# Sliding-window attention with a gated mix: maxima and output blocks stored in one transfer each, attention features ordered by row number and then head, reciprocals as one repeated block

## The chip, the cores and the metric

The kernel runs on one core of one Trainium2 chip. The metric is the time of one execution on the device in microseconds (us); the smaller the better. A core has a matrix engine (PE, whose weight loads are shown apart as PEld), a vector engine (DVE), a scalar engine (ACT), a general engine (POOL) and a sequencer that here issues every transfer between the chip's memory (DRAM) and the core's memory (SP).

## The reference

`x` has 2048 rows (tokens) of 512 features. One branch is attention with 32 heads of 16 features, in which a token sees itself and the 255 tokens before it; the other is a gated feed-forward block with 1376 inner features. A gate of one number per token mixes the two.

```python
qkv = (x @ wqkv).reshape(B, S, 3, H, Dh)           # H = 32, Dh = 16
scores = jnp.einsum("bhqd,bhkd->bhqk", q, k) * (Dh ** -0.5)
mask = (idx[:, None] - idx[None, :] >= 0) & (idx[:, None] - idx[None, :] < 256)
p = softmax(where(mask, scores, -1e9)); o = einsum("bhqk,bhkd->bhqd", p, v)
a = o.reshape(B, S, D) @ wo
b = (sigmoid(x @ w_gate) * (x @ w_up)) @ w_down
out = g * a + (1 - g) * b                          # g = sigmoid((x * gate_w).sum(-1))
```

## The kernel before

All matrix products are made in float32 by splitting each operand into a high and a low part and adding three products (`mm3`, lines 88 to 91). The program has two long stages, which follow one another on PE.

**Attention (about 40 to 553 us).** The 32 heads form 8 groups of four, and each group has 16 blocks of 128 tokens, so that there are 128 units. The loop `for u in range(N)` (line 763) takes one unit per turn. In turn `u` the scores of unit `u` are computed once to find each query's maximum (`s_part`, line 331: PE at L340, DVE's maximum at L346). The scores of unit `u - 9` are computed a second time, transposed and with the maximum already subtracted (`st_part`, line 380: PE at L390, then ACT's exponential at L395). Between these, PE fills up with pieces of the projections and of the feed-forward block's first products (L273). Every fourth turn a burst of products with the values is done (`pv_burst`, L454).

The maximum travels from the first computation to the second through DRAM, once for four blocks, which gives 32 rounds. A round goes like this:

1. DVE splits the negated maxima into a high and a low part and transposes them in 32 x 32 squares into a tile `nt` of 128 x 32 (`max_split`, L358 to L362).
2. SP stores `nt` to `max_scratch` (`max_store`, L369): four transfers, one for each square of 32 partitions.
3. SP waits until these have landed and loads them back as rows of the operand tiles `ring` (`max_load`, L374). For round `s` this stands in turn 4s + 5.
4. `st_part` reads them, for the first time in turn 4s + 7 (in turn 4s + 9 where a group begins).

SP works through one list in order. What is issued in a turn is written in the loop: the load of maxima, then what the turn before has put into `later` (stores of computed tiles, L315), then up to three of the copies that build the next operand tile (`ring<-sh`, `ring<-sl`, also L315, `SD = 3`), then other loads; the store of maxima comes in the middle of the turn (L833). A transfer that has to wait holds up all those behind it.

**An output block.** After the last burst of a chunk of 512 tokens, `o_take` (line 462) holds four heads in a tile `ob` of 128 x 512: head `hh` has rows 32 hh to 32 hh + 31, of which the first 16 are the head's features and row 16 is the sum of the softmax (a column of ones stands beside the values). The rest is not used. Four transfers store the features to `oT_scratch` and a fifth stores the four rows of sums to `sum_scratch`.

**Down projection (about 553 us to the end).** For each chunk of 512 tokens (`c`) there are 11 steps (`f`), numbered `n` through all chunks, each of 12 matrix products `pd`; then 48 products `pa` with `wo` for the attention. A step reads a tile `hb`, which is made two to three steps ahead from two loads of `gu_scratch` (`h_load`, L686), a sigmoid (ACT, L703), a product (DVE, L704) and a split (`h_skew`; ACT at L85, DVE at L86). At the end of the attention loop `sums_load` (L713) reads the sums of a chunk, `sums_invert` takes the reciprocals (L717), and they are stored to `rec_scratch`. For each block of 128 tokens `o_load` (line 887) reads the features of all heads and their reciprocals. `o_scale` (line 895) spreads each head's reciprocal over the partitions of its 16 features with a shuffle (L897) and multiplies (L898).

Of the kernel before, what the change touches and what calls it, by code (L numbers as in the profile page):

```python
# [7 lines left out]
F32 = mybir.dt.float32  # L8
# [3 lines left out]
ALU = mybir.AluOpType  # L12
PSUM = bass.MemoryType.PSUM

P = 128
T = 2048
D = 512
ND = D // P
H = 32
DH = 16  # L20
HG = 4
NG = H // HG
CH = 512
NC = T // CH
# [26 lines left out]
QB = 32  # L51
# [12 lines left out]
def gated_mix_kernel(  # L64
# [14 lines left out]
    nc = tc.nc  # L79
# [10 lines left out]
        mm(ps, lh, rl, start=False, stop=False)  # L90
        mm(ps, ll, rh, start=False, stop=last)  # L91

    oT_d = nc.dram_tensor("oT_scratch", (D, T), F32, kind="Internal").ap()
    sum_d = nc.dram_tensor("sum_scratch", (NC, H, CH), F32, kind="Internal").ap()
    rec_d = nc.dram_tensor("rec_scratch", (NC, H, CH), F32, kind="Internal").ap()
    gu_d = nc.dram_tensor("gu_scratch", (2, NF, P, T), F32, kind="Internal").ap()
    v_d = nc.dram_tensor("v_scratch", (NB, P, VROW), F32, kind="Internal").ap()
# [39 lines left out]
    with ExitStack() as actx:  # L137
# [8 lines left out]
        later = []  # L146
# [218 lines left out]
        def max_store(s):  # L365
            nt = nms.pop(s)
            dst = max_d[s].rearrange("h l b (a t) -> a (h l b) t", t=QB)
            for a in range(P // QB):
                nc.sync.dma_start(dst[a], nt[a * QB:(a + 1) * QB])  # L369

        def max_load(s):
            st = ring[s // 2 % RING].bitcast(F32).rearrange("(a r) j f -> r a j f", r=QB)
# [89 lines left out]
        def o_take(g, i, n, acc):  # L462
            s = g * NC + i // 4
            if i % 4 == 0:
                obs[s] = cpool.tile([P, CH], F32, tag="ob", name=f"ob{s}", bufs=2)
            part = obs[s][:, i % 4 * P:(i % 4 + n) * P]
            lo = 64 if i == 0 else 0
            nc.scalar.copy(part, acc[0][:, 0:n * P])

            def rest():  # L470
                nc.vector.tensor_tensor(part[:, lo:], acc[1][:, lo:n * P], part[:, lo:], op=ALU.add)
                if (i + n) % 4:
                    return
                ob, c = obs.pop(s), i // 4
                for hh in range(HG):
                    h = g * HG + hh
                    later.append((oT_d[h * DH:(h + 1) * DH, c * CH:(c + 1) * CH], ob[32 * hh:32 * hh + DH]))
                later.append((sum_d[c, g * HG:(g + 1) * HG], ob.rearrange("(h r) f -> r h f", r=32)[DH]))

            behind.insert(0, rest)  # L480

# [78 lines left out]
        def gu_mm(f, c, w, k, half=None):  # L560
            fw = width(f, w)
            if (f, c, w) not in gp:
                gp[f, c, w] = ps.tile([P, CH], F32, tag="misc", name=f"gu{f}_{c}_{w}", bufs=3)
            wh, wl = (gv[:, 0, w], gv[:, 1, w]) if f < NF - 1 else wq[NG]
            group_mm(gp[f, c, w], fw, wh, wl, c, k, half)
# [17 lines left out]
        def proj_out(s):  # L583
# [5 lines left out]
                lambda k, h=None, a=(f, c, w): gu_mm(*a, k, h),  # L589
# [116 lines left out]
        sm = {}  # L706

        def flat(v, c):
            return v[c].rearrange("h (q t) -> (h q) t", t=P)

        def sums_load(c):
            sm[c] = cpool.tile([P, P], F32, tag="sm", name=f"sm{c}", bufs=2)
            nc.sync.dma_start(sm[c], flat(sum_d, c))  # L713

        def sums_invert(c):
            t = sm.pop(c)
# [39 lines left out]
        w = 0  # L756
# [6 lines left out]
        for u in range(N):  # L763
# [49 lines left out]
            for hh in range(HG):  # L813
                if hh == 0 and u % 2 == 0:
                    if u in bursts:
                        pv_burst(*bursts[u])
                if hh == 0:
                    head = min(2, bursts.get(u, (0, 0))[1] // 2)
                    run_slots(head)
                if u < NU:  # L820
                    s_part(u, hh)
                if 0 <= u - LAG < NU:
                    st_part(u - LAG, hh ^ 1 if u < NU else hh)
                if u < LAG:
                    flush(behind)
                    run_slots(GAP)
                    flush(acts)
                else:
                    if behind:
                        behind.pop(0)()  # L830
                    if acts:
                        acts.pop(0)()
                if hh == 2 and u % 4 == 0 and 0 < u <= NU:  # L833
                    max_store(u // 4 - 1)
                if u >= LAG:
                    run_slots((LAST[hh] if u >= NU else GAPS[u % 4][hh] if u > LAG + 2 else GAP * (u % 2 == 0 or hh < HG - 1)) - (hh < head))
# [10 lines left out]
            if SUMS <= u and (u - SUMS) % 4 == 0:  # L847
                sums_load((u - SUMS) // 4)
# [13 lines left out]
        def slot(h, d, c):  # L862
            return (xh, xl)[h][:, d, c * CH:(c + 1) * CH]

        def blocks(v):
            return v.rearrange("p (d t) -> p d t", d=ND)

        def free_slot(h, d, c):
            return slot(h, d, c).bitcast(F32)

        spread = [w - w % DH for w in range(QB)]
        oh = [blocks(slot(0, t, 1)) for t in range(4)]
        ol = [blocks(slot(1, t, 1)) for t in range(4)]
        o_raw = [blocks(free_slot(1, k, 2)) for k in range(2)]
# [1 line left out]
            region[:, SPARE + 3 * CH * k:SPARE + 3 * CH * (k + 1)].rearrange("p (n t) -> p n t", t=CH) for k in range(2)  # L876
        ]
        wide = [blocks(spare[k][:, 2]) for k in range(2)]
        rows = [blocks(free_slot(0, k, 3)) for k in range(2)]
        accs = [spare[k % 2][:, k // 2] for k in range(4)]  # L880

        def gate(c):
# [3 lines left out]

        def o_load(b):
            c, t = divmod(b, 4)
            nc.sync.dma_start(o_raw[b % 2], oT_d[:, b * P:(b + 1) * P].rearrange("(d p) t -> p d t", p=P))
            nc.sync.dma_start(  # L890
                rows[b % 2].rearrange("(h w) d t -> w h d t", w=DH)[0],
                rec_d[c, :, t * P:(t + 1) * P].rearrange("(d h) t -> h d t", d=ND),
            )

        def o_scale(b):
            o, w = o_raw[b % 2], wide[b % 2]
            nc.vector.stream_shuffle(w, rows[b % 2], spread)  # L897
            nc.vector.tensor_tensor(w, o, w, op=ALU.mult)  # L898

        def o_split(b):  # L900
            split(oh[b % 4], ol[b % 4], wide[b % 2])
# [1 line left out]
        for n, (c, f) in enumerate(steps):  # L903
# [22 lines left out]
            if 1 <= f < 9 and f % 2 == 1:  # L926
                o_load(4 * c + f // 2)
            if 3 <= f and f % 2 == 1:
                o_scale(4 * c + f // 2 - 1)
# [9 lines left out]
            for t in range(4):  # L939
                b = 4 * c + t  # L940
# [17 lines left out]
def _layout(inputs):  # L958
    import numpy as np

    x = np.asarray(inputs["A_x"]).reshape(T, D)
    wqkv = np.asarray(inputs["A_wqkv"])
    wqk = wqkv[:, :2 * D].reshape(ND, P, 2, NG, HG * DH).transpose(3, 1, 0, 2, 4).reshape(NG, P, ND, P)
    wg = np.asarray(inputs["B_w_gate"])
    wu = np.asarray(inputs["B_w_up"])
    nf = F // P
    gu = np.stack([wg, wu]).reshape(2, ND, P, F)
    main = gu[..., :nf * P].reshape(2, ND, P, nf, P).transpose(3, 0, 2, 1, 4)
    tail = gu[..., nf * P:].transpose(0, 2, 1, 3)
    last = np.concatenate([tail[1], tail[0, ..., :GL]], axis=2)  # L970
    return {
        "xT": x.T.reshape(ND, P, NC, CH).transpose(2, 0, 1, 3),
        "wqk": wqk,
        "wv": wqkv[:, 2 * D:],
        "wo": np.asarray(inputs["A_wo"]),
        "wgu": main,
        "wgu_last": last,
        "wg_last": tail[0, ..., GL:],
        "wd": np.asarray(inputs["B_w_down"]),
        "gw": np.asarray(inputs["gate_w"]).reshape(1, D),  # L980
        "x": x,
    }
# [23 lines left out]
```

## Time and profile before

| | |
|---|---|
| time, median of 3 runs | 721.82 us (721.75 to 722.55) |
| the profiled execution: its time / its span | 724.11 us / 722.4 us |
| PE busy | 715.6 us, 99% of the span |
| DVE / ACT / POOL busy | 66% / 60% / 24% |
| granted clock of PE | 1.0 of full speed in all slices |
| DMA engines, mean busy share | 54.5% of 16 engines' span by the SP queue's packets |

The span goes from the first to the last instruction of the profiled execution. An engine is busy while one of its instructions runs; the ends of matrix products are modelled, so that a busy PE may still hide short stalls.

### The profile page before, as it was taken

Reading aid. Unit: us, or ns where it says so; the run is one execution under the profiler, and the core shown is the slowest. Engines: PE = TensorE matmul, PEld = TensorE weight load, DVE = VectorE, ACT = ScalarE, POOL = GpSimd, SP = SyncE. Lnnn points to the kernel's source line nnn. Section 1 sums busy time; section 2 is a strip of 40 time slices with the busy share of each in tenths; the row PEclk is TensorE's granted clock in tenths of the full one; section 3 lists DMA queues with packets and bytes.
Section 4 is the critical chain, followed back from the end, with each engine's and each line's share of the span. In section 5 each row is a group of like instructions: output and inputs, shape, how many; then the busy total and the mean of one; then the engine's idle time right before and its main releaser. Section 6 shows DMA issues by size and latency. Waiting matters only on the chain.

```text
span 722.4 us, 20457 instructions
## 1 busy us (share of the span) xinstructions
PE 715.6 (99%) x7759; PEld 588.6 (81%) x7759; DVE 478.7 (66%) x1473; ACT 432.9 (60%) x889; POOL 169.9 (24%) x257
## 2 busy tenths in 40 slices
PE   9999999999999999999999999999999999999997
PEld 7689788888878888888788888888887888888886
DVE  5458777657766676766677667676566868576571
ACT  6413776667667677666667767767675635435241
POOL 7000333332233223333223323332331000000000
PEclk9999999999999999999999999999999999999999
DMA  9456554645355455443555525556475959377541
GB/s 325 106 155 196 162 131 125 164 134 153 97 137 150 124 145 146 136 133 98 140 162 138 139 88 161 162 152 201 161 238 183 311 185 317 147 242 234 174 115 59
DMA packets 89322, 117.93 MB, mean 163 GB/s; under 512 B 33870, under 2 KB 43726, under 8 KB 89224
## 3 DMA queue, kind: packets, MB, share of 16 engines
q1 hardware_dynamic: 89224, 116.62, 54.5%
q8 instruction: 61, 1.00, 0.6%
q14 instruction: 37, 0.30, 0.1%
HBM read 54.70 MB, written 36.71 MB: 127 GB/s over the span
## 4 chain that ended last, share of the span: by engine, by line
PE 99%; DMA 0%; issue 0%; DVE 0%; ACT 0%; DVEq 0%
PE gu L273 35%; PE pj L273 10%; PE pvs L454 8%; PE s L340 6%; PE st L390 6%; PE pd L89 6%; PE pd L91 6%; PE pd L90 6%; PE vps L254 4%; PE pa L89 2%; PE pa L91 2%; PE pa L90 2%; PE pvst L454 2%; PE gl L498 1%; PE vps L89 1%; PE vps L90 1%
## 5 line engine op out<-in xcount | busy, mean ns | idle before, releaser
L346 DVE CUSTOM_DVE_ANT_0 junk<-s,mask 128x384 f32<-128x384 f32 (+2 forms) x512 | 267.5, 531 | 142.8 <-PE st L390 92.1
L273 PE MATMUL gu<-xh,w 64*128 64x512 f32 x1264 | 330.9, 395 | 0.0
L395 ACT ACTIVATE region<-st 128x384 f32<-128x384 f32 (+2 forms) x512 | 242.6, 476 | 93.2 <-PE st L390 47.2
L273 PE MATMUL gu<-xl,w 64*128 64x512 f32 x632 | 225.7, 393 | 0.0
L273 PEld LDWEIGHTS gu<-xh,w 64*128 64x128 f32 x1264 | 188.0, 185 | 19.1 <-issue 6.1
L390 PE MATMUL st<-ring 64*128 64x384 f32 (+2 forms) x536 | 167.6, 320 | 1.2 <-DMA ring<-max_scratch 1.1
L340 PE MATMUL s<-ring 64*128 64x384 f32 (+2 forms) x536 | 167.8, 321 | 0.0
L400 POOL TENSOR_SCALAR_AFFINE_SELECT region<-region 128x512 f32<-128x512 f32 x128 | 86.8, 678 | 332.9 <-ACT region L395 293.8
L273 PEld LDWEIGHTS gu<-xl,w 64*128 64x128 f32 x632 | 113.8, 185 | 4.1
L340 PEld LDWEIGHTS s<-ring 64*128 64x128 f32 x536 | 98.6, 184 | 21.5 <-DVE mx L346 12.1
L390 PEld LDWEIGHTS st<-ring 64*128 64x128 f32 x536 | 98.3, 184 | 8.6 <-DMA ring<-max_scratch 1.4
L273 PE MATMUL pj<-xl,wqh 64*128 64x512 f32 (+1 forms) x240 | 95.5, 402 | 0.0
L273 PE MATMUL pj<-xh,wqh 64*128 64x512 f32 (+1 forms) x240 | 93.6, 395 | 0.0
L273 PE MATMUL pj<-xh,wql 64*128 64x512 f32 (+1 forms) x240 | 75.2, 392 | 0.0
L405 POOL TENSOR_SCALAR_AFFINE_SELECT region<-region 128x512 f32<-128x512 f32 x112 | 73.9, 660 | 0.0
L454 PE MATMUL pvs<-region,vg 64*32 64x320 f32 (+4 forms) x1408 | 71.5, 344 | 0.1
L454 PE MATMUL pvst<-region,vg 64*32 64x320 f32 (+4 forms) x1408 | 70.0, 340 | 0.0
L89 PE MATMUL pd<-ring,hb 128*128 128x512 f32 (+1 forms) x176 | 69.4, 395 | 0.0
L91 PE MATMUL pd<-ring,hb 128*128 128x512 f32 (+1 forms) x176 | 68.9, 392 | 0.0
L90 PE MATMUL pd<-ring,hb 128*128 128x512 f32 (+1 forms) x176 | 68.4, 389 | 0.0
L454 PEld LDWEIGHTS pvs<-region,vg 64*32 64x32 f32 x1408 | 44.4, 106 | 25.4 <-issue 4.2
L85 ACT CAST hb<-region 128x512 fp32r<-128x512 f32 (+1 forms) x36 | 22.4, 622 | 53.7 <-DVE region L704 41.4
(117 smaller groups left out, 1136.5 us busy)
## 6 DMA issues: line engine op xcount, KB each, us to landing
gu_scratch<-sp SPq DMA_DIRECT2D x79, 256.0 KB
region<-gu_scratch SPq DMA_DIRECT2D x68, 256.0 KB
ring<-sh SPq DMA_DIRECT2D x128, 128.0 KB
ring<-sl SPq DMA_DIRECT2D x64, 128.0 KB
guraw<-in_wgu_dram SPq DMA_DIRECT2D x20, 256.0 KB
v_scratch<-region SPq DMA_DIRECT2D x16, 272.0 KB
vg<-v_scratch SPq DMA_DIRECT2D x8, 544.0 KB
region<-in_xT_dram SPq DMA_DIRECT2D x16, 256.0 KB
```

What stands on the lines that cost most here:

```text
L89: mm(ps, lh, rh, start=first, stop=False)
L90: mm(ps, lh, rl, start=False, stop=False)
L91: mm(ps, ll, rh, start=False, stop=last)
L254: mm(vp[b], (xl if w == 1 else xh)[r, d, b * P:(b + 1) * P], (wvl if w == 2 else wvh)[r, d], start=k == 0 and half == 0, stop=k == 3 * ND ...
L273: mm(pt[0:fw], (wl if w == 2 else wh)[r, d], (xl if w == 1 else xh)[r, d, c * CH:(c + 1) * CH], start=k == 0 and half != 1, stop=k == 3 * ...
L340: mm(pt[:, (k - k0) * P:(e - k0) * P], lhsT, blk(g, k, hh, 1, e - k), start=k == k0, stop=e == i + 1, skip_group_check=True,)
L346: nc.vector.tensor_tensor_reduce(junk[:, 0:n], pt[:, 0:n], mask[:, 3 * P - n:], scale=1.0, scalar=NEG, op0=ALU.add, op1=ALU.max, accum_out ...
L390: mm(pt[:, (q - j) * P:(e - j) * P], lhsT, blk(g, q, hh, 0, e - q), start=q == j, stop=e == last, skip_group_check=True,)
L395: nc.scalar.activation(pts[u][:, hh, 0:n], pt[:, 0:n], AF.Exp, scale=SCALE)
L400: nc.gpsimd.affine_select(p[:, :, 0:P], p[:, :, 0:P], pattern=[[0, HG], [1, P]], compare_op=ALU.is_ge, fill=0.0, base=0, channel_multiplie ...
L405: nc.gpsimd.affine_select(p[:, :, 2 * P:], p[:, :, 2 * P:], pattern=[[0, HG], [-1, P]], compare_op=ALU.is_gt, fill=0.0, base=0, channel_mu ...
L454: mm(acc[half][32 * hh:32 * hh + 32, q0:q1], vr[r, c:c + 32], pts[g * NB + j][r, hh, q0 + o:q1 + o], start=m == 0, stop=m == len(order[0]) ...
```

## The change

The store of maxima is one transfer of all 128 partitions. An output block is stored in one transfer too: all 128 rows of `ob`, with the sums and the 15 unused rows of each head, into an `oT_scratch` that is now ordered by row number (0 to 31), then head, then token. The sums are row 16 of it, and `sums_load` reads them from there. In `o_load` a partition now holds one row number and one head (head = partition modulo 32), so that the reciprocals of a block of 128 tokens are the same 32 rows, repeated four times down the partitions and the same for all four tiles of features. They are loaded so, and the multiplication reads them with a repeated index; the shuffle goes. The rows of `wo` are put in the same order on the host.

```diff
-    oT_d = nc.dram_tensor("oT_scratch", (D, T), F32, kind="Internal").ap()
-    sum_d = nc.dram_tensor("sum_scratch", (NC, H, CH), F32, kind="Internal").ap()
+    oT_d = nc.dram_tensor("oT_scratch", (QB, H, T), F32, kind="Internal").ap()
...
             dst = max_d[s].rearrange("h l b (a t) -> a (h l b) t", t=QB)
-            for a in range(P // QB):
-                nc.sync.dma_start(dst[a], nt[a * QB:(a + 1) * QB])
+            nc.sync.dma_start(dst, nt)
...
                 ob, c = obs.pop(s), i // 4
-                for hh in range(HG):
-                    h = g * HG + hh
-                    later.append((oT_d[h * DH:(h + 1) * DH, c * CH:(c + 1) * CH], ob[32 * hh:32 * hh + DH]))
-                later.append((sum_d[c, g * HG:(g + 1) * HG], ob.rearrange("(h r) f -> r h f", r=32)[DH]))
+                dst = oT_d[:, g * HG:(g + 1) * HG, c * CH:(c + 1) * CH]
+                later.append((dst.rearrange("r h t -> h r t"), ob))
...
-            nc.sync.dma_start(sm[c], flat(sum_d, c))
+            nc.sync.dma_start(sm[c], oT_d[DH, :, c * CH:(c + 1) * CH].rearrange("h (q t) -> h q t", t=P))
...
-        rows = [blocks(free_slot(0, k, 3)) for k in range(2)]
+        rows = [free_slot(0, k, 3)[:, 0:P] for k in range(2)]
...
-            nc.sync.dma_start(o_raw[b % 2], oT_d[:, b * P:(b + 1) * P].rearrange("(d p) t -> p d t", p=P))
-            nc.sync.dma_start(
-                rows[b % 2].rearrange("(h w) d t -> w h d t", w=DH)[0],
-                rec_d[c, :, t * P:(t + 1) * P].rearrange("(d h) t -> h d t", d=ND),
-            )
+            heads = oT_d[0:DH].rearrange("r h t -> (r h) t")[:, b * P:(b + 1) * P]
+            nc.sync.dma_start(o_raw[b % 2], heads.rearrange("(d p) t -> p d t", p=P))
+            nc.sync.dma_start(rows[b % 2], rec_d[c, :, t * P:(t + 1) * P].partition_broadcast(P // H))
...
             o, w = o_raw[b % 2], wide[b % 2]
-            nc.vector.stream_shuffle(w, rows[b % 2], spread)
-            nc.vector.tensor_tensor(w, o, w, op=ALU.mult)
+            r, _ = bass.broadcast_tensor_aps(rows[b % 2].rearrange("p (o t) -> p o t", o=1), o)
+            nc.vector.tensor_tensor(w, o, r, op=ALU.mult)
...
-        "wo": np.asarray(inputs["A_wo"]),
+        "wo": np.asarray(inputs["A_wo"]).reshape(H, DH, D).transpose(1, 0, 2).reshape(D, D),
```

The order of the instructions on PE, ACT and POOL is the same as before. On SP the transfers keep their order and 224 of them go. These are SP's transfers before the change from the load of maxima of round 9 to that of round 10 (a row gives line, destination, source and shape, and how many in a row):

```order
L374 DMA ring<-max_scratch 4x2x512
L315 DMA gu_scratch<-sp_2_1_3131 128x512
L315 DMA ring<-fill_scratch 4x2x1024
L315 DMA ring<-sh_2739 32x1024 x2
L315 DMA gu_scratch<-sp_3_1_3192 128x512
L315 DMA ring<-sh_2739 32x1024 x3
L315 DMA oT_scratch<-ob_3260 16x512 x4
L315 DMA sum_scratch<-ob_3260 4x512
L315 DMA ring<-sh_2739 32x1024 x3
L315 DMA ring<-sl_2740 32x1024 x3
L538 DMA guraw_0_3402<-in_wgu_dram 128x512
L369 DMA max_scratch<-nt_3383 32x32 x4
```

The same place after the change:

```order
L372 DMA ring<-max_scratch 4x2x512
L314 DMA gu_scratch<-sp_2_1_3073 128x512
L314 DMA ring<-fill_scratch 4x2x1024
L314 DMA ring<-sh_2691 32x1024 x2
L314 DMA gu_scratch<-sp_3_1_3134 128x512
L314 DMA ring<-sh_2691 32x1024 x3
L314 DMA oT_scratch<-ob_3202 4x32x512
L314 DMA ring<-sh_2691 32x1024 x3
L314 DMA ring<-sl_2692 32x1024 x3
L534 DMA guraw_0_3340<-in_wgu_dram 128x512
L367 DMA max_scratch<-nt_3321 4x32x32
```

Five transfers of the block ahead of the store of maxima have become one, and so have the four of the store itself.

At the end of the attention loop, SP before the change issues the last output block, the last chunk's sums and the loads for step 5 and later ones:

```order
L315 DMA oT_scratch<-ob_10155 16x512 x4
L315 DMA sum_scratch<-ob_10155 4x512
L713 DMA sm_10281<-sum_scratch 128x128
L686 DMA region<-gu_scratch 128x512 x2
L123 DMA wdraw_10290<-in_wd_dram 128x512
```

After the change the load of sums reads what the one transfer has written, and so waits for all of it:

```order
L314 DMA oT_scratch<-ob_9935 4x32x512
L709 DMA sm_10057<-oT_scratch 128x1x128
L682 DMA region<-gu_scratch 128x512 x2
L122 DMA wdraw_10066<-in_wd_dram 128x512
L682 DMA region<-gu_scratch 128x512 x2
```

The loads of steps 5 and 6 stand behind it as before.

## Rows read from the trace of the kernel before

**Rows 1.** The page, span and part 1: busy time of each engine.

```profile
span 722.4 us, 20457 instructions
...
PE 715.6 (99%) x7759; PEld 588.6 (81%) x7759; DVE 478.7 (66%) x1473; ACT 432.9 (60%) x889; POOL 169.9 (24%) x257
```

**Rows 2.** Busy time by stretch: stretch, its length, PE, PEld, DVE, ACT, POOL, clock.

```profile
0.00:20.00 20.00, 18.75 (x80) 15.97 (x81) 9.27 (x15) 11.82 (x19) 13.77 (x13) 1.00 0.83 295
...
210.00:270.00 60.00, 58.87 (x810) 48.65 (x808) 40.64 (x150) 40.50 (x89) 19.46 (x30) 1.00 0.51 140
...
680.00:722.40 42.40, 38.11 (x167) 30.99 (x165) 20.68 (x36) 13.79 (x24) 0.00 (x0) 1.00 0.38 119
```

**Rows 3.** Chain that ended last, 200 to 216 us: start, us, what.

```profile
209.47 2.42 DMA ring<-max_scratch
```

**Rows 4.** Waits: engine, line, releaser; us in total, times, longest.

```profile
PEld st L390 <- DMA ring<-max_scratch: 1.4, 1, 1.4
```

**Rows 5.** Timeline of SP, rounds 9 to 10: start, us of issue, transfers.

```profile
198.00 1.91 SPq L315 DMA_DIRECT2D oT_scratch<-ob  x4
199.96 0.56 SPq L315 DMA_DIRECT2D sum_scratch<-ob  x1
...
204.62 0.34 SPq L538 DMA_DIRECT2D guraw<-in_wgu_dram  x1
205.08 1.78 SPq L369 DMA_DIRECT2D max_scratch<-nt  x4
209.47 0.59 SPq L374 DMA_DIRECT2D ring<-max_scratch  x1
```

**Rows 6.** Timeline of DVE: the transpose of round 10.

```profile
201.31 0.21 DVE L362 STREAM_TRANSPOSE nt<-nm 128x32 f32<-128x32 f32 x1
```

**Rows 7.** SP's issues by tensor: ns of one (least/median/most), first and last start.

```profile
L369 SPq DMA_DIRECT2D max_scratch<-nt x128: 302/419/2049, 59.3 to 518.3; - x128
L374 SPq DMA_DIRECT2D ring<-max_scratch x32: 552/582/596, 64.1 to 520.5; - x32
L315 SPq DMA_DIRECT2D oT_scratch<-ob x128: 302/420/1289, 89.5 to 555.5; - x128
L315 SPq DMA_DIRECT2D sum_scratch<-ob x32: 509/561/734, 91.2 to 556.0; - x32
```

**Rows 8.** Timeline of SP, round 17.

```profile
307.37 1.71 SPq L369 DMA_DIRECT2D max_scratch<-nt  x4
310.24 0.58 SPq L374 DMA_DIRECT2D ring<-max_scratch  x1
```

**Rows 9.** The page, part 3: packets, MB, share of 16 engines' span.

```profile
q1 hardware_dynamic: 89224, 116.62, 54.5%
```

**Rows 10.** Timeline of SP, round 3, and of PEld two turns later.

```profile
89.48 1.71 SPq L315 DMA_DIRECT2D oT_scratch<-ob  x4
...
94.06 1.73 SPq L424 DMA_DIRECT2D vg<-v_scratch  x2
...
103.04 0.58 SPq L374 DMA_DIRECT2D ring<-max_scratch  x1
...
105.31 0.18 PEld L390 LDWEIGHTS st<-ring 64*128 64x128 f32 x1
```

**Rows 11.** Timelines of SP, PE, ACT and DVE around the first steps.

```profile
553.16 0.50 PE L89 MATMUL pd<-ring,hb 128*128 128x512 f32 x1
554.23 1.69 SPq L315 DMA_DIRECT2D oT_scratch<-ob  x4
557.66 0.34 SPq L713 DMA_DIRECT2D sm<-sum_scratch  x1
561.68 0.63 ACT L703 ACTIVATE region<-region 128x512 f32<-128x512 f32 x1 [1.14 <-DMA region<-gu_scratch]
567.58 0.68 DVE L86 TENSOR_TENSOR hb<-region,hb 128x512 fp32r<-128x512 f32 x1
```

**Rows 12.** Groups by line on DVE: the shuffle of `o_scale`.

```profile
L897 DVE STREAM_SHUFFLE region<-xh 128x512 f32<-128x512 f32 x16 | 11.8, 739 | 0.0
```

More of the change, by code (lines that the diff above doesn't have):

```diff
@@ L869, in free_slot @@
             return slot(h, d, c).bitcast(F32)
-        spread = [w - w % DH for w in range(QB)]
         oh = [blocks(slot(0, t, 1)) for t in range(4)]
```

## Prediction

> **What bounds the kernel now.** I read the busy times first. PE is busy for 715.6 of 722.4 us, and no other engine comes near it [rows 1]. So only what PE waits for can shorten this kernel, and all of its idle time together is 6.8 us. The busy times by stretch say where these 6.8 us lie [rows 2]: 1.25 us before PE starts (20.00 - 18.75), 1.13 us between 210 and 270 us (60.00 - 58.87) and 4.29 us at the end (42.40 - 38.11), when PE has finished and the last rows are added and stored. That makes 6.67, and the rest, some 0.1 us, is spread thinly. The first and the last piece hold none of the changed lines. What can be won by taking waits from PE is therefore little more than the 1.13 us in the middle.
>
> The chain of work shows what this piece is: at 209.47 us it passes from PE to the load of maxima of round 10, which takes 2.42 us to land [rows 3]. The list of waits has the same event once: PE's weight load for the second scores waited 1.4 us for a load of maxima, and this is the only such wait [rows 4]. So 31 of the 32 rounds of maxima are in time and one is late.
>
> Why that one is late is told by SP. The transposed maxima of round 10 were ready at 201.31 + 0.21 = 201.52 us [rows 6], but their store was issued at 205.08, 3.56 us later, and the load at 209.47 [rows 5]. SP was behind: it came to the store only after an output block (five transfers, 198.00 to 200.52) and the copies and the load behind it.
>
> **The change, part by part.**
>
> *SP's issues.* Per round the store of maxima is four issues of 0.42 us, some 1.71 us with the gaps [rows 7, 8]. The new form has three dimensions and is not in the trace; the nearest row is the load of maxima, also 4 by something by a row, with 0.58 us an issue [rows 7]. Below, a plain form costs 0.42, so the bounds are 0.42 to 0.6, and I take 0.58. That saves 1.13 us of SP per round. An output block is 4 x 0.42 + 0.56, with gaps 2.5 us (198.00 to 200.52, [rows 5]); as one issue of 0.58 it saves 1.9 us. Over 32 rounds SP gives up about 97 us. By itself this is worth nothing, because PE does not wait for SP, only for what lands late; the cover is PE's own queue of work.
>
> *Round 10.* SP's list ahead of the store gets shorter by 1.9 us (the block), so the store can be issued at 205.08 - 1.9 = 203.2 instead of 205.08, still after the transpose at 201.52. It ends at 203.8. Between the end of an undisturbed store and the load behind it lie 310.24 - 309.08 = 1.16 us [rows 8]. To this comes the data of one transfer of 128 short rows. The SP queue's packets take 0.545 x 16 x 722.4 us / 89224 = 71 ns each on the average, at 1307 bytes [rows 9]. If the 128 rows of 128 bytes spread over 16 engines, 8 of them add at most 0.6 us; if only four engines carry them (the outermost size of the transfer is 4), 32 packets add at most 2.3 us, and at the mean rate per byte 0.2 us. I take 0.5 us, nearer to the rate per byte, as the rows are a tenth of a mean packet. The load is then issued at 203.8 + 1.16 + 0.5 = 205.5 us (205.0 to 207.3) against 209.47, and lands 2.42 us later at 207.9 (207.4 to 209.7). PE's weights asked for it 1.4 us before 209.47 + 2.42 = 211.9, that is at 210.5. Even the late end is in time. **This takes the wait away: -1.13 us by PE's idle time, -1.4 us by its weight load's; I take -1.13.**
>
> *Round 3, the round with least to spare.* Its load is issued at 103.04, so by 2.42 us it lands at about 105.4, and the weights of the second scores that come at 105.31 started without a recorded wait [rows 10]. There is nothing left over. Ahead of its store stand the two loads of values issued at 94.06, and they wait for a store of values that stands behind the output block issued at 89.48. The block now carries 128 rows of 2 KB instead of 68. At the mean rate of 1307 / 71 = 18.5 bytes per ns, 256 KB take 0.9 us over 16 engines and 3.5 us over four. In the second case the store of values may land later by up to 3.5 us less the 2.4 us that SP saves ahead of it, some 1 us. Against that the store of maxima is one issue instead of 3.45 us of four. I put this at 0, bounds 0 to +1 us.
>
> *The extra bytes.* 60 more rows of 2 KB in 32 blocks are 3.9 MB on top of 116.62, 3%, on engines that are half busy [rows 9]. Cost 0, as no other load is waited for in attention; bounded by the round 3 case.
>
> *The end of the loop.* The last load of sums now waits for the whole block. Issued at 554.23, the block lands by the prices above at 554.23 + 0.58 + 1.16 + 0.9 to 3.5 = 556.9 to 559.5 us; the load of sums left at 557.66 so far [rows 11]. It is 0 to 1.8 us later, and so are the loads for steps 5, 6 and 7 that stand behind it on SP. The sigmoid of step 5 waits for its load already, until 561.68 [rows 11]. Who waits next is PE at step 6: its tile was ready at 567.58 + 0.68 = 568.3. A step is 12 products of 38.11 us / 167 = 0.228 us [rows 2], 2.74 us, so step 6 begins at about 553.16 + 0.3 + 6 x 2.74 = 569.9. There are 1.6 us to spare, and 0.74 us more, since one shuffle goes from ahead of that tile on DVE [rows 12]. A delay of 1.8 us fits into 2.3. Cost 0.
>
> *The shuffles.* 16 of 739 ns, 11.8 us of DVE [rows 12], all after 560 us, where DVE is not waited for; the multiplication stays, and how its repeated operand is read costs little if anything. Worth 0 to PE. The loads of reciprocals have 128 rows instead of 32, and stand two steps ahead of their use; 0.
>
> **A page that speaks against it.** The row above knows only the mean packet and not over how many engines one transfer goes; the shapes say that the outermost size of both new stores is 4. The Trainium skill, page "DMA: Bandwidth & Descriptors", section "Rules for kernel authors", says that an outermost dimension smaller than 16, a leading repeated one among them, keeps a transfer on at most that many of the 16 engines. By that rule the three new transfers run on four engines, and the upper of each pair of numbers above holds: 3.5 us for a block and not 0.9. No row here shows a transfer's engines. By the sum even this stays hidden.
>
> **Sum.** -1.13 + 0 + 0 + 0: the profiled span would be 721.3 us. The profiled execution took 724.11 us, 1.7 us more than its span and 2.29 more than the median of the runs shown; I take the gain off the median: 721.82 - 1.13 = 720.7 us. For this kernel 0.2%, or 1.44 us, is about what a measurement tells from no change, so this counts as no change.
>
> **The rivals.**
>
> *There is no such wait in the timed runs* (0.25). The profiled execution is 2.29 us slower than the median, and late landings may belong to it. For: it is a single wait in 32 rounds, and it rests on SP's being behind. Against: SP's order and the issue times are the same in every run. Then nothing changes: 721.8 us.
>
> *Slower: the block's store holds up what stands behind it* (0.12). The place is the load of sums at 557.66. It decides once the last block lands more than about 2.3 us later than the sums did, at about 560; from there each us goes to PE through step 6. If four engines carry the block and their packets take twice the mean (another 3.5 us), the delay is 5.3 us and PE waits 3.0: 721.82 - 1.13 + 3.0 = 723.7 us. A milder form is round 3's wait of 1 us: 721.7. For: the outermost size. Against: the engines are half idle. This is the case that the page's rule makes more likely; the trace has no row for it.
>
> *More than the one wait* (0.08). The timed runs lie up to 0.8 us apart, so waits of this kind may be longer or come twice there. Two of 1.4 us: 719.0 us; with the small pieces of idle time, 1.4 + 0.1 = 1.5: 720.3.
>
> *The forecast* has 0.55, at 720.2 to 721.2.
>
> **The range.** Of these, 719.6 to 722.7 us leaves out the far part of the slower case and of the better one, some 0.13; its ends also cover the 0.8 us by which the timed runs differ. The likeliest case's own range is 720.2 to 721.2. Faster by over 0.2% means under 720.4: most of the third rival and a third of the forecast, 0.24. Slower by over 0.2% means over 723.3: 0.09. The same: 0.67.
>
> **What would show it.** In the changed kernel's profile the list of waits should have no load of maxima ahead of PE, the stretch from 210 to 270 us should show PE busy all through, the issues of both stores should be near 0.58 us, and the load of maxima of round 10 should leave SP about 4 us earlier. Right in the time but wrong in the reason would be a PE that waits elsewhere in attention. The prediction is wrong if step 5 or 6 begins late after 557 us, if round 3's second scores wait for their maxima, or if the store of maxima takes more than 4 us to land.

## The result, and the profile after

The changed kernel takes 732.08 us (median of 4 runs, 731.98 to 732.19) against 722.14 us of the kernel before (4 runs, 721.75 to 722.55). The ratio is 1.0139, with a 95% interval of 1.0126 to 1.0151: it is slower by 10.0 us (9.1 to 10.9). The prediction was 720.7 us, no change, with a range that ended at 722.7. It was wrong.

The profiled execution after took 732.02 us. Its span and busy times, from the page (before: [rows 1]):

```profile
span 730.0 us, 20048 instructions
PE 719.0 (98%) x7759; PEld 590.9 (81%) x7759; DVE 468.4 (64%) x1441; ACT 432.5 (59%) x889; POOL 168.7 (23%) x257
```

The span grew by 7.6 us. PE is idle for 4.2 us more (11.0 against 6.8) and busy for 3.4 us more, although it does the same 7759 products. So there are two things to find: new waits, and products that take longer. (The timed medians differ by 2.3 us more than the spans: the profiled execution of before was 2.0 us above the median of its runs, and the time outside the span is 0.3 us longer after. The loss is the timed one, 10.0 us; the two spans show 7.6 of it.)

The waits of PE after:

```profile
PE pvs L452 <- DMA vg<-v_scratch: 2.5, 1, 2.5
PE pd L89 <- ACT hb L85: 2.3, 1, 2.3
...
PE gu L272 <- ACT sp L566: 0.6, 1, 0.6
```

The wait for a load of maxima [rows 4] is gone, as predicted. Three others have come: one for the values (2.5), one in the down projection (2.3), one in the feed-forward products (0.6). The stretches in which they lie (columns as in [rows 2]):

```profile
90.00:150.00 60.00, 57.54 (x762) 48.56 (x768) 40.31 (x146) 38.92 (x85) 17.84 (x29) 0.97 0.55 139
210.00:270.00 60.00, 60.00 (x840) 49.00 (x832) 41.69 (x152) 41.63 (x90) 19.78 (x31) 1.00 0.53 146
510.00:530.00 20.00, 19.37 (x283) 16.30 (x264) 11.12 (x32) 13.70 (x29) 5.62 (x10) 1.00 0.52 157
560.00:600.00 40.00, 37.69 (x157) 30.20 (x157) 24.88 (x42) 19.51 (x35) 0.00 (x0) 0.96 0.80 248
```

From 210 to 270 us PE is now busy throughout; before, it lost 1.13 us there [rows 2]. In two of the other three stretches the granted clock is below 1.00. That is where the longer products are: 3% of 60 us and 4% of 40 us make 1.8 + 1.6 = 3.4 us. A finer table of the first place shows the lowered clock in the slice in which PE stood still and in the next one (1.00 is the upper of the clock's two levels, 2.4 GHz, and 0.50 the lower, 1.2 GHz, so that 0.73 is a slice spent partly at the lower one):

```profile
100.00:105.00 5.00, 3.22 (x73) 2.64 (x81) 0.00 (x0) 0.39 (x1) 1.18 (x2) 0.73 0.63 113
105.00:110.00 5.00, 5.00 (x73) 3.87 (x56) 3.15 (x10) 3.01 (x6) 0.33 (x1) 0.93 0.48 139
110.00:115.00 5.00, 5.00 (x50) 4.56 (x47) 4.08 (x18) 3.83 (x10) 2.11 (x4) 1.00 0.72 172
```

In slices of 1 us the order is plainer: the clock was still 1.00 while PE stood, from 99.32 to 101.78 us, fell only after PE had started again, was 0.50 from 103 to 105 us and 1.00 again from 106 us.

What is late at the first place can be read from SP's timeline (before: [rows 10]):

```profile
89.49 0.59 SPq L314 DMA_DIRECT2D oT_scratch<-ob  x1
90.18 0.41 SPq L314 DMA_DIRECT2D v_scratch<-region  x1
95.90 1.75 SPq L422 DMA_DIRECT2D vg<-v_scratch  x2
```

The block is one issue of 0.59 us instead of 2.3. The store of values behind it is therefore issued sooner than before, yet the loads that wait for that store are issued at 95.90 instead of 94.06. So the store behind the block lands late. At the end of the attention loop the chain of work (start, us, what) has the block itself:

```profile
553.56 5.82 DMA gu_scratch<-two_sum
559.44 6.46 DMA oT_scratch<-ob
565.91 0.57 SPq L709
566.59 0.53 SPq L682
567.21 4.08 DMA region<-gu_scratch
...
572.16 0.63 ACT hb L85
```

It takes 6.46 us from issue to landing. The load of sums (L709) waits for it, the loads of step 5 (L682) stand behind that, and PE waits for step 5's tile. SP's waits for transfers show late blocks ahead of all four loads of sums (us in total, times, longest):

```profile
SPq L709 <- DMA oT_scratch<-ob: 22.1, 4, 6.4
SPq L422 <- DMA v_scratch<-region: 5.2, 1, 5.2
```

and the same two waits in the kernel before:

```profile
SPq L713 <- DMA sum_scratch<-ob: 3.8, 4, 1.5
SPq L424 <- DMA v_scratch<-region: 1.7, 1, 1.7
```

The four loads of sums now wait 18.3 us longer in all, and the loads of values 3.5.

### The profile page after: what moved, and what is told of

It reads as the page before. It is cut to its first block, busy times and chain, and to the rows that moved or that the text cites. A ratio compares the mean times of both kernels' runs of the same rounds, so it can differ in the third digit from the quotient of the medians.

```text
span 730.0 us, 20048 instructions
## 1 busy us (share of the span) xinstructions
PE 719.0 (98%) x7759; PEld 590.9 (81%) x7759; DVE 468.4 (64%) x1441; ACT 432.5 (59%) x889; POOL 168.7 (23%) x257
## 4 chain that ended last, share of the span: by engine, by line
PE 94%; DMA 4%; ACT 1%; DVE 0%; issue 0%; SPq 0%; ACTq 0%; DVEq 0%
PE gu L272 32%; PE pj L272 11%; PE pvs L452 8%; PE s L339 6%; PE st L388 5%; PE pd L91 5%; PE pd L89 5%; PE pd L90 5%; PE vps L253 4%; PE pa L91 2%; PE pa L89 2%; PE pa L90 2%; PE pvst L452 2%; DMA gu_scratch<-sp 1%; PE gl L494 1%; DMA oT_scratch<-ob 1%
## 5 line engine op out<-in xcount | busy, mean ns | idle before, releaser
L452 PE MATMUL pvs<-region,vg 64*32 64x320 f32 (+4 forms) x1408 | 73.3, 350 | 2.6 <-DMA vg<-v_scratch 2.5
L89 PE MATMUL pd<-ring,hb 128*128 128x512 f32 (+1 forms) x176 | 70.0, 397 | 2.3 <-ACT hb L85 2.3
L452 PE MATMUL pvst<-region,vg 64*32 64x320 f32 (+4 forms) x1408 | 71.6, 346 | 0.0
L91 PE MATMUL pd<-ring,hb 128*128 128x512 f32 (+1 forms) x176 | 69.8, 397 | 0.0
L90 PE MATMUL pd<-ring,hb 128*128 128x512 f32 (+1 forms) x176 | 69.1, 392 | 0.0
L452 PEld LDWEIGHTS pvs<-region,vg 64*32 64x32 f32 x1408 | 46.1, 108 | 28.0 <-issue 7.0
L466 ACT COPY ob<-pvs 128x512 f32<-128x512 f32 (+1 forms) x34 | 19.1, 561 | 58.7 <-PE pvst L452 47.1
```

Of the source, the lines that this page charges most:

```text
L89: mm(ps, lh, rh, start=first, stop=False)
L452: mm(acc[half][32 * hh:32 * hh + 32, q0:q1], vr[r, c:c + 32], pts[g * NB + j][r, hh, q0 + o:q1 + o], start=m == 0, stop=m == len(order[0]) ...
```

## The experiments

The theory (A in the expectations): one transfer of a block, whose outermost size is 4 (the first number of its shape, 4 x 32 x 512), lands late, and what stands behind it on SP pays. Its rivals: the distance between the rows (B), the store of maxima (C), the repeated load of reciprocals (D). "Loss" below is (ratio - 1) x 722 us, with its 95% interval; after has 10.0.

**Maxima alone.** The kernel before, with this edit only:

```diff
-            for a in range(P // QB):
-                nc.sync.dma_start(dst[a], nt[a * QB:(a + 1) * QB])
+            nc.sync.dma_start(dst, nt)
```

> The kernel before with one edit: the maxima of a round are stored in one transfer; output blocks, their layout and the reciprocals as before. Theory A (the block stored in one transfer with an outermost size of 4 lands 6 to 8 us after its issue, and what queues behind it on SP is late): nothing of the loss appears, and round 10's wait of 1.13 us goes: about 721.0 us (722.14 - 1.13). Theory B (256 KB between the rows of the block's destination, or the extra bytes): the same, 721.0. Theory C (the one-transfer store of maxima delays the loads behind it): most of the 9.9 us appears, about 730. Theory D (the reciprocals, loaded repeated and late at the end): 721.0.

Measured: 721.34 us, ratio 0.9990 (0.9981 to 0.9999). SP's timeline in round 10 (before: [rows 5]) and PE's stretch there:

```profile
201.49 0.59 SPq L368 DMA_DIRECT2D max_scratch<-nt  x1
204.08 0.55 SPq L373 DMA_DIRECT2D ring<-max_scratch  x1
...
210.00:270.00 60.00, 60.00 (x821) 49.46 (x822) 42.06 (x155) 41.98 (x91) 19.39 (x30) 1.00 0.48 134
```

The load leaves SP 5.4 us sooner than before and the wait is gone. This half of the change brings what was predicted of the whole, and C falls. (It does so in another way than predicted; see "Why the prediction was wrong".) It is also the one version in this study whose interval lies below 1.

**The block in four transfers.** After, with the same bytes to the same places:

```diff
-                later.append((dst.rearrange("r h t -> h r t"), ob))
+                for hh in range(HG):
+                    later.append((dst[:, hh], ob[32 * hh:32 * hh + 32]))
```

> The changed kernel, but each output block goes out as four transfers of 32 rows, with the same bytes to the same places; maxima in one transfer, reciprocals repeated as in the changed kernel. Theory A: the four transfers land within about 3 us of the first issue, as the five did before, and the waits at 100 us (2.5), 520 us (0.6) and 570 us (2.3) and the lowered clock behind them go: 721 to 722 us. Theory B: the pitch of 256 KB and the bytes are the same, so it stays near 732. Theory C: 732. Theory D: only the loss at the end stays, some 4 us, about 726.

Measured: 722.02 us, ratio 1.0000 (0.9991 to 1.0008). The whole loss is gone. SP's timeline at the first place, and its wait for blocks:

```profile
89.63 1.75 SPq L314 DMA_DIRECT2D oT_scratch<-ob  x4
91.47 0.37 SPq L314 DMA_DIRECT2D v_scratch<-region  x1
93.64 1.76 SPq L422 DMA_DIRECT2D vg<-v_scratch  x2
...
SPq L710 <- DMA oT_scratch<-ob: 6.2, 7, 2.5
```

The store of values is issued 1.3 us later than after the change, and the loads that wait for it 2.3 us sooner. The extra bytes and the 256 KB between rows are still there, so they alone cost nothing that can be measured; D can't be the main cause.

**The block alone.** After, with the maxima in four transfers as before (the first diff, reversed).

> The changed kernel, but the maxima stored in four transfers as before. Theory A: the loss stays, and round 10's wait may come back: 732 to 733 us. Theory B: 732 to 733. Theory C: the loss goes, about 722. Theory D: 732 to 733, so this run tells only C from the rest, and shows what the maxima's own edit is worth beside a late block.

Measured: 734.89 us, ratio 1.0176 (1.0139 to 1.0213), with six runs from 729.87 to 742.35; without the longest their median is 733.66. The profiled execution took 740.47 us. PE's waits in it:

```profile
PE pd L89 <- ACT hb L85: 3.2, 1, 3.2
PE pvs L453 <- DMA vg<-v_scratch: 2.7, 1, 2.7
PE st L389 <- DMA ring<-max_scratch: 2.6, 1, 2.6
```

The block carries the loss: even the shortest run lies above the longest of the kernel before (724.10). A wait for maxima comes back in this execution, longer than in the kernel before, at about 338 us and not in round 10; whether the time is above that of after is not certain (the intervals overlap).

**Shape against row distance.** The scratch is ordered by head, then row number, so that rows stand 8 KB apart. Without a gap the 128 rows join into one dimension; with an unused row behind each head they stay 4 x 32; with one behind each 16 rows, 8 x 16.

```diff
-    oT_d = nc.dram_tensor("oT_scratch", (QB, H, T), F32, kind="Internal").ap()
+    oT_d = nc.dram_tensor("oT_scratch", (H, QB, T), F32, kind="Internal").ap()              # no gap
+    oT_d = nc.dram_tensor("oT_scratch", (H, QB + 1, T), F32, kind="Internal").ap()          # size 4
+    oT_d = nc.dram_tensor("oT_scratch", (2 * H, QB // 2 + 1, T), F32, kind="Internal").ap() # size 8
```

The features are loaded in four transfers per block of 128 tokens in all three.

> The changed kernel with the scratch of outputs ordered by head, then row number: a block is still one transfer of 128 rows of 2 KB, 256 KB in all, but its rows stand 8 KB apart and its outermost size is 128; the features of a block of 128 tokens are loaded in four transfers of 128 short rows, the reciprocals in one that repeats each row four times side by side, and the rows of wo are put in the order that this gives. Theory A: the block lands in about 2.5 us and the three waits go: about 721 us. Theory B: the pitch is 8 KB as before the change, so that part goes as well: 721; what the bytes alone cost stays. Theory C: 732. Theory D: the reciprocals are still one repeated transfer, with four loads ahead of it instead of one, so a loss at the end of 4 us or more stays: 726.

> As the version with the scratch ordered by head and then row number (e4), but with one unused row behind each head's 32, so that the four heads of a block no longer join into 128 rows at one distance: the transfer keeps an outermost size of 4, with the rows of a head 8 KB apart. Bytes, order on SP and everything else as in e4. Theory A (the shape with outermost size 4 makes the block late): the block lands 6 to 8 us after its issue again and the loss comes back, 730 to 735 us. Theory B (the pitch of 256 KB does): 722.0 as e4.

> As the version with a gap behind each head's 32 rows (e5, outermost size 4, 729.67 us), but with a gap behind each 16 rows, so that the block's one transfer has an outermost size of 8: 8 x 16 x 512, same bytes, same order on SP, rows 8 KB apart. If the time in which a block lands falls with the outermost size, the four waits of SP for a block, 19.9 us together with size 4 and 9.7 with 128, come to 12 to 14 us, PE's wait at 100 us shrinks from 2.4 us to under 1, and the time is 722 to 725. If any gap between the rows costs the same: 729.7 again.

Measured: no gap 722.00 us, ratio 0.9996 (0.9987 to 1.0005); size 4 729.67 us, 1.0110 (1.0094 to 1.0127); size 8 723.41 us, 1.0012 (1.0003 to 1.0020). SP's waits for blocks, of no gap, size 4 and size 8 in this order, and under them PE's wait at the first place with size 4:

```profile
SPq L709 <- DMA oT_scratch<-ob: 9.7, 4, 3.8
...
SPq L709 <- DMA oT_scratch<-ob: 19.9, 4, 5.8
...
SPq L709 <- DMA oT_scratch<-ob: 12.8, 4, 4.2
...
PE pvs L452 <- DMA vg<-v_scratch: 2.4, 1, 2.4
```

One transfer of 256 KB is no loss if its rows form one dimension. The same bytes at the same distance lose 7.9 us (6.8 to 9.2) when a gap of one row keeps the outermost size at 4, and 0.9 (0.2 to 1.4) at 8. So the shape is what costs, and B falls as the main cause. The Trainium skill, page "DMA: Bandwidth & Descriptors", section "Rules for kernel authors", says that an outermost dimension below 16 keeps a transfer on at most that many of the 16 engines. The order of the three sizes agrees with it; over how many engines a transfer went, no view here shows. That size 4 loses 2.1 us less here than in the change may come from the distance or from the four loads; this stays open.

**Where the loss is made.** After, with four transfers for some blocks only (`s` numbers the blocks; the first is 0, the last four are those of the last group).

```diff
+                if s == 0:              # second run: s >= NSTEP - 4; third: either
+                    for hh in range(HG):
+                        later.append((dst[:, hh], ob[32 * hh:32 * hh + 32]))
+                else:
+                    later.append((dst.rearrange("r h t -> h r t"), ob))
```

> The changed kernel, with the first output block alone (the one at 89.5 us) stored in four transfers of 32 rows. Theory A: the wait for the values at 101.8 us (2.46 us) and the lowered clock behind it (3% of 60 us, 1.8 us) go, the places at 520 and 570 us stay: 732.1 - 4.3 = 727.8 us. If the lowered clock is not a consequence of the wait, only 2.5 us go: 729.6.

> The changed kernel, with the blocks of the last group alone (those behind 500 us, four of 32) stored in four transfers each. Theory A: the waits at 520 us (0.63) and 570 us (2.3) and the lowered clock behind the latter (4% of 40 us, 1.6 us) go, the place at 100 us stays: 732.1 - 4.5 = 727.6 us. If the end's loss comes from the repeated load of reciprocals (theory D): 730 to 732.

> The changed kernel with the first block and the four of the last group stored in four transfers each; the other 27 blocks go out in one transfer as in the change. If the late blocks cost something only at the places seen in the trace: as with all blocks in four, 722.0 us. If they cost something everywhere, a little at a time (contention with other transfers): 27 of 32 of what the first block and the last group don't explain, so above 723.

Measured: first block 726.60 us, ratio 1.0059 (1.0047 to 1.0071); last four 725.94, 1.0058 (1.0044 to 1.0073); all five 722.98, 1.0007 (0.9997 to 1.0016). The stretches from 90 and from 560 us, of the first and under it of the second:

```profile
90.00:150.00 60.00, 60.00 (x827) 50.00 (x825) 42.40 (x156) 42.33 (x92) 18.90 (x30) 1.00 0.58 147
560.00:600.00 40.00, 37.80 (x158) 30.28 (x157) 24.77 (x43) 17.29 (x31) 0.00 (x0) 0.96 0.80 244
...
90.00:150.00 60.00, 57.19 (x776) 47.97 (x780) 39.34 (x145) 38.80 (x84) 18.64 (x30) 0.97 0.55 141
560.00:600.00 40.00, 39.24 (x172) 31.89 (x172) 27.34 (x47) 18.75 (x34) 0.00 (x0) 1.00 0.81 242
```

Each mended place has its busy time and its clock back (a wait of 0.8 us stays at the end), and the other place keeps its stop and its lowered clock. The first place alone loses 4.2 us (second run), the end with the place at 520 us 4.3 (first run); from the trace of after they were 2.5 + 1.8 = 4.3 and 0.6 + 2.3 + 1.6 = 4.5. That is 8.5 of the 10.0, and the rest is within the intervals. The 27 blocks that stay in one transfer in the third run cost nothing that can be told from 0.5 us (-0.2 to 1.2).

**What queues behind the block.** Here all blocks stay in one transfer, and only SP's order changes. In the first run the first block goes behind the two loads of values; in the second, the last load of sums goes behind step 5's loads as well.

```diff
-                later.append((dst.rearrange("r h t -> h r t"), ob))
+                (held if s == 0 else later).append((dst.rearrange("r h t -> h r t"), ob))
...
                 v_load(0)
+                later.extend(held)
```

```diff
-            if SUMS <= u and (u - SUMS) % 4 == 0:
+            if SUMS <= u < N - 1 and (u - SUMS) % 4 == 0:
                 sums_load((u - SUMS) // 4)
...
                 h_load(n + AHEAD)
+            if n == 0:
+                sums_load(NC - 1)
```

> The changed kernel, with the first output block's one transfer moved on SP from ahead of the last store of values to behind the two loads of values; nothing else is changed. If the loss at 100 us is a matter of the queue (the store of values and with it the loads of values stand behind a block that lands late), it goes as when that block is stored in four: 727.8 us, unless the maxima of the next round, which are now behind the block, come late in turn (then up to 732). If the block delays whatever moves at the time, wherever it stands in the list: 732.

> The changed kernel with all blocks in one transfer, and two moves on SP: the first block behind the loads of values (as e9, 726.66 us), and the last load of sums, which waits for the last block, behind the two loads of step 5. If the loss at the end is a matter of the queue (step 5's loads stand behind a load that waits), PE's wait of 2.1 us in step 5 and the lowered clock behind it, 1.6 us, go: 723.0 us. If step 6's loads, which still stand behind it, come late in turn: 725 to 727.

Measured: first 726.66 us, ratio 1.0064 (1.0051 to 1.0077); second 725.84, 1.0062 (1.0048 to 1.0077). SP's timeline of the first run:

```profile
89.77 0.33 SPq L315 DMA_DIRECT2D v_scratch<-region  x1
92.12 1.90 SPq L423 DMA_DIRECT2D vg<-v_scratch  x2
94.12 1.96 SPq L315 DMA_DIRECT2D oT_scratch<-ob  x1
```

With the block out of its way the store of values lets its loads go at 92.12, and PE's wait for values is gone: the same gain as from splitting that block (4.6 against 4.3 left). So at the first place it is a matter of the queue. At the end the same reasoning failed: the second move brings nothing that can be told from the first alone (4.5 us left, 3.5 to 5.6). PE's waits there, and the chain:

```profile
PE pd L91 <- DVE hb L86: 1.4, 2, 0.9
PE pd L89 <- ACT hb L85: 0.9, 1, 0.9
...
553.37 7.54 DMA oT_scratch<-ob
...
563.65 5.01 DMA xh<-rec_scratch
568.67 6.27 DMA xh<-rec_scratch
575.07 0.69 DVE region L893
575.76 0.61 DVE hb L86
```

Step 5's loads no longer stand behind the load of sums, and PE's one stop of 2.1 us became three of at most 0.9. But the loads of reciprocals and of later steps still stand there, and DVE, which multiplies by the reciprocals ahead of its part of a later tile, comes late in turn. Between 560 and 600 us PE lost 2.3 us instead of 2.9. Most of the wait moved on; it did not go. So at the end the queue is argued from the chain and not shown by a move; that the shape of the blocks makes the loss there is shown by the run with the last four in four transfers.

**The reciprocals.** The blocks in four transfers (second experiment), with the reciprocals in four transfers of 32 rows too:

```diff
-            nc.sync.dma_start(rows[b % 2], rec_d[c, :, t * P:(t + 1) * P].partition_broadcast(P // H))
+            for k in range(P // H):
+                nc.sync.dma_start(rows[b % 2][k * H:(k + 1) * H], rec_d[c, :, t * P:(t + 1) * P])
```

> All blocks in four transfers of 32 rows (as e2), and the reciprocals of a block of 128 tokens loaded in four transfers of 32 rows instead of one that repeats them. If the repeated load is what is left of the loss at the end (DVE waited 9.1 us for it in e2, and PE 0.5): the wait of DVE goes below 2 us and the time to that of the maxima alone, 721.3. If not: 722.0 as e2.

Measured: 722.50 us, ratio 1.0002 (0.9993 to 1.0010), no gain. DVE still waits for them as in the second experiment (9.1 us):

```profile
DVE region L893 <- DMA xh<-rec_scratch: 8.9, 12, 1.1
```

So it isn't the repeat that makes them late, and D falls. In the kernel before DVE waited 0.3 us for them. What makes the difference is open (in all these versions the reciprocals of a block of 128 tokens are 128 rows, before 32, and no run here varies that); in the versions whose blocks land in time (the second experiment, this one, and the scratch by heads without a gap) PE waited 0.2 to 0.8 us in the down projection.

## Why the prediction was wrong

**Round 10: the number right, the way not.** The wait went, as "-1.13" said, and shows by itself in the maxima alone (-0.7 us, -1.4 to -0.1). But the prediction freed the store by "1.9 us (the block)", and in the maxima alone the block is still five transfers. There the store left 3.6 us sooner (201.49 against 205.08, [rows 5]) because round 9's load of maxima had left 3.6 us sooner (before, and under it the maxima alone):

```profile
191.31 0.58 SPq L374 DMA_DIRECT2D ring<-max_scratch  x1
...
187.71 0.55 SPq L373 DMA_DIRECT2D ring<-max_scratch  x1
```

From this load to the store of round 10 SP took 13.8 us in both. What held SP up before was that round 9's load left 5.1 us behind its four stores (issued at 186.25), against 2.0 us behind the one store (at 185.68); the block ahead of round 10 is not needed to explain it. Why round 9's stores took so long is open. That the gain came out near the forecast is in this part luck. The issue of the new store was priced at 0.58 us and takes that in the median, though up to 1.77:

```profile
L367 SPq DMA_DIRECT2D max_scratch<-nt x32: 522/578/1772, 60.0 to 522.5; - x32
```

Taken out of a total of +10.0, it is a small part.

**The price of a block: too low, and its upper end too.** The step "256 KB take 0.9 us over 16 engines and 3.5 us over four" gave 2.6 to 5.2 us from issue to landing. The chain has 6.46 us after and 7.54 in the last of the moved versions. The four-engine price was made with the mean packet of the whole queue; why the block takes 1.2 to 2.3 us more than that, no run shows.

**Round 3, the failed step at the first place.** The prediction named the right queue: the store of values behind the block, and the loads of values behind that store. But it asked only whether the maxima, which come later still, would be in time, and set "0, bounds 0 to +1 us". It did not ask who reads the values. The loads of values left 1.8 us later (95.90 against 94.06). The values are read by a burst of products (`pv_burst`), PE came to it at 99.32 us and stood until 101.78, and the place cost 4.2 us (3.2 to 5.3).

**The end of the loop, the second failed step.** In "A delay of 1.8 us fits into 2.3" the delay was mis-sized, and the room was that of step 6 alone. The load of sums left 4.50 us behind the start of step 0 before (557.66 - 553.16, [rows 11]) and leaves 9.43 behind it after (565.91 - 556.48): 4.9 us later. Of these 3.0 are the block's landing (6.47 against 3.43 us from its first issue) and 1.9 are that the block is issued later itself, which the chain puts down to a store of the feed-forward branch that took 5.82 us. The wait came at step 5, and not at step 6: the prediction saw that step 5's sigmoid waits for its load, but went on to "Who waits next is PE at step 6". Before, the high part of step 5's tile was ready 3.3 us ahead of its use (563.75 and 567.03 us). After, it comes 5.7 us later against step 0 (572.78 - 556.48, before 563.75 - 553.16), and PE waits 2.3.

**A third place was missing.** At 512.68 us a block stands ahead of a store of the feed-forward branch. The chain of after shows what follows:

```profile
512.61 0.58 ACT sp L566
513.30 7.48 DMA gu_scratch<-sp
520.88 0.59 ACT sp L566
```

The store, though its own rows are 128, takes 7.48 us; ACT waits for its buffer, and PE for ACT: 0.6 us.

**The clock was not priced.** The sum counted waits alone. The granted clock was 1.00 in every stretch before [rows 2], so nothing there showed that a stop of PE has a price beyond its length. After, two stops of 2.5 and 2.3 us came with 3.4 us of slower products. It does not always follow: in the version with the first block moved PE stopped 2.1 us at the end, and the clock stayed at 1.00 in the profiled execution. Nor is it shown that the lowered clock adds its whole length to the time: with the first block in four, a run with a mean granted clock of 1.000 took 726.64 us and one with 0.998 (some 1.4 us of lost clock) 726.77; with the last four in four, 725.49 and 725.36.

**What held.** No gain shows from SP's saved issues or from the shuffles, and no cost from the extra 3.9 MB: with the same bytes in four transfers the time is 722.0 us, that of the kernel before. Of the signs of being wrong that the prediction named, step 5 began late, and one store of maxima took more than 4 us to land (SP waited 4.8 us for it near 490 us), though PE did not wait for it. The load of maxima of round 10 left SP 1.2 us earlier (208.32 against 209.47) and not about 4, since PE had by then lost the time at the first place.

**The rivals.** The slower rival had the mechanism, a block's store that holds up what stands behind it, at one of the three places and at 723.7 us; it got 0.12. The rule of the Trainium skill that was weighed speaks for exactly this, and the runs with size 4, 8 and 128 agree with it in their order. The prediction set it aside with "By the sum even this stays hidden", and that sum had looked for what a late block costs in two places only: at the maxima of round 3, and at step 6.

## What to carry to other kernels

Fewer issues are not a cheaper transfer: what counts is how soon it lands, and a form with a small outermost size (4 here) can land several us later than the same bytes in four pieces, or in one whose rows form one dimension. When a transfer may land late, list all that stand behind it in its queue, and ask of each who reads it and when, not only of the one with the least room before. Of 32 blocks in one transfer five did the damage; splitting those gave all but 0.5 us back, and moving only the first behind the loads that mattered gave back about half.

## What the hardware showed that was not expected

A transfer that is issued sooner can land later because of the one ahead of it in the same queue: the store of values, issued at 90.18 us behind a block of 4 x 32 rows, let its loads go at 95.90; issued at 91.47 behind the same block in four pieces, at 93.64; and issued at 89.77 ahead of the block, at 92.12. And the products that follow a wait of PE can be slower: after the 2.5 us stop that ended at 101.78 us the granted clock fell to 0.50 and was back at 1.00 by 106 us, which in that execution took some 1.8 us; the 1.13 us stop of the kernel before left it at 1.00.
